# Converting the float64 weights of a fused kernel: sign on GpSimd, low bits as 16-bit halves, one subtraction moved

## The chip, the cores and the metric

The kernel runs on one core of one Trainium2 chip. Its time is device microseconds of one execution; the figure for a kernel is the median of several runs. A trace taken by the hardware profiler on one execution lies beside the times, and all rows below come from it. The engines are TensorE (PE for its matmuls, PEld for its weight loads), VectorE (DVE), ScalarE (ACT), GpSimd (POOL) and SyncE (SP, which issues most DMAs).

## The reference

Three layers follow one another. Linear attention over 8 batches, 8 heads, 576 positions and 64 channels: a softmax of q over channels, a softmax of k over positions, `kv = k^T v`, then `q kv`. The result, 4608 tokens of 512 channels, goes through a feed-forward layer: `h = x @ w_in` (512 to 2048), `g = s * relu(h)^2 + b`, `y = g @ w_out` (2048 to 512). Then a mixture of 8 experts: each token goes to the one expert with the highest cosine similarity, through `relu(x @ w1[e]) @ w2[e]`, times its softmax weight.

What matters here: `w_in` and `w_out` arrive as float64. No engine of this kernel works in float64, so the kernel itself turns every weight into a float32 by bit operations on its two 32-bit words: the sign is the top bit of the high word, exponent and the first 20 mantissa bits come from the high word, and the last three mantissa bits are the top three bits of the low word.

## The kernel before

Work is in blocks. The feed-forward layer runs over 12 token tiles of 384 (index `t`) and, inside each, over 16 blocks of 128 hidden columns (index `m`). Per block, `emit_l1` (lines 483 to 485) multiplies each weight tile three times, high part by high, high by low, low by high, because a float32 is split into two parts `fp32r`, a rounded high part and the rest. `emit_g` squares and scales on ScalarE (lines 496 to 509), `emit_l2` (lines 524 to 528) multiplies by `w_out`. In the first tile, `t = 0`, blocks 0 to 13 take `w_out` unsplit: line 524 reads the converted float32 weights, the tile named `cxout`, directly. Only from block 14 on is the split pair (`wout`) read, lines 526 to 528.

Weights are converted while `t = 0` runs. There are 16 pieces of 128x1024 values, eight of `w_in` (`in 0` to `in 7`) and eight of `w_out`, in the order in 0, in 1, out 0, in 2, out 1, and so on. A piece takes these instructions:

- `conv_load`: SP loads the raw float64 words, two loads of 512 KB, into the tile `rawin` or `rawout`.
- `conv_a`: ScalarE takes the absolute value of the high word and rescales it into `ct` (line 162); VectorE shifts the low word right by 29 and writes all 32 bits of `x` (line 163), then writes the sign into the upper 16-bit half of `x` (line 164). `x` is the tile `cxin` or `cxout`, of which there are two each.
- `conv_b`: VectorE shifts `ct` left by three and ORs it with `x` (line 171), ScalarE rounds the result to the high part (line 175).
- `conv_c`: VectorE subtracts the high part to get the low part (line 179).

`conv_first` does this for in 0 inside the opening section, where attention of batch 0 and tile 0 is computed. `conv_step` does it for the others: at each `m` of tile 0, half 0 issues a load and `conv_b` of the piece before, half 1 issues `conv_a` of the next piece and `conv_c` of the piece before.

Beside this, attention for the next tile and batch is computed in small steps by generators (`attn_k`, `attn_q`), in places fixed by tables. In `attn_k` VectorE reduces a maximum (lines 255 to 262), PE transposes it (line 267), VectorE reduces again (line 270), PE spreads it back (line 273), VectorE subtracts it (lines 292 and 294), ScalarE takes the exponential (lines 299 and 300) and PE multiplies by v (line 311). Each engine runs its instructions in the order in which the program issues them; an instruction that waits holds up all that stand behind it on its engine. `consts_late`, at the end of tile 0, fills small constants and the token table on GpSimd (lines 117 to 138).

Of the kernel before, what the change touches and what calls it, by code (L numbers as in the profile page):

```python
# [8 lines left out]
F32 = mybir.dt.float32  # L9
F32R = mybir.dt.float32r  # L10
BF16 = mybir.dt.bfloat16
I32 = mybir.dt.int32
U16 = mybir.dt.uint16
ALU = mybir.AluOpType
# [11 lines left out]
NM = DFF // 128  # L26
# [23 lines left out]

GLB = 2
IDLE = {(1, 0): 26}
LATE = {(7, 2): 1, (6, 3): 2, (2, 1): 1, (5, 3): 2, (7, 0): 2, (4, 1): 2, (6, 1): 2, (5, 2): 2, (1, 1): 2, (4, 3): 1, (3, 1): 2, (7, 3): 2, (3, 0): 1, (2, 0): 2, (1, 3): 1}


@with_exitstack
def attn_ffn_moe(ctx: ExitStack, tc: tile.TileContext, q, k, v, w_in, w_out, s_in, b_in,
                 emb, tau, w1, w2, out, ysc=None):
    nc = tc.nc
# [13 lines left out]
    sp = stage.enter_context(tc.tile_pool(name="sp", bufs=2, side="right"))  # L73
# [11 lines left out]
    def wpair(dtype, name):  # L85

        return wp.tile([128, 2, 1024], dtype, tag="w", name=name)
# [53 lines left out]
    wt = {}  # L141
    raw_t = {}
    conv_t = {}
    full = {}

    def conv_load(kind, i):

        r = wpair(I32, f"raw{kind}{i}")
        for n in range(2):
            nc.sync.dma_start(out=r[:, n, :], in_=(w_in if kind == "in" else w_out)[2 * i + n])  # L150
        raw_t[kind, i] = r

    def conv_a(kind, i):

        t = sp.tile([128, 1024], I32, tag="ct", name="ct", bufs=1)
        room = "in" if (kind, i) == ("out", NM // 2 - 1) else kind
        x = sp.tile([128, 1024], I32, tag="cx" + room, name="cx" + kind)
        raw = raw_t.pop((kind, i)).rearrange("p n c -> p (n c)")
        r = raw.rearrange("p (f two) -> p f two", two=2)
        r16 = raw.bitcast(U16).rearrange("p (f four) -> p f four", four=4)  # L160
        x16 = x.bitcast(U16).rearrange("p (f two) -> p f two", two=2)
        nc.scalar.activation(out=t.bitcast(F32), in_=r[:, :, 1].bitcast(F32), func=AF.Abs, scale=2.0 ** -112)
        nc.vector.tensor_scalar(out=x, in0=r[:, :, 0], scalar1=29, scalar2=None, op0=ALU.logical_shift_right)
        nc.vector.tensor_scalar(out=x16[:, :, 1], in0=r16[:, :, 3], scalar1=0x8000, scalar2=None,
                                op0=ALU.bitwise_and)
        conv_t[kind, i] = (t, x)

    def conv_b(kind, i):

        t, x = conv_t.pop((kind, i))  # L170
        nc.vector.scalar_tensor_tensor(out=x, in0=t, scalar=3, in1=x,
                                       op0=ALU.logical_shift_left, op1=ALU.bitwise_or)
        full[kind, i] = x.bitcast(F32)
        wt[kind, i] = wpair(F32R, f"w{kind}{i}")
        nc.scalar.activation(out=wt[kind, i][:, 0, :], in_=full[kind, i], func=AF.Copy)

    def conv_c(kind, i):
        w = wt[kind, i]
        nc.vector.tensor_tensor(out=w[:, 1, :], in0=full[kind, i], in1=w[:, 0, :].bitcast(F32), op=ALU.subtract)

    def w_of(kind, m):

# [45 lines left out]
    def idle(n, o=None):  # L228

        if o is None:  # L230
            o = ps_h()
        z = ident.bitcast(BF16)
        for _ in range(n):
            nc.tensor.matmul(o[:, 256:512], z[:, 0:128], z, start=True, stop=True)
# [13 lines left out]
    def attn_k(b, j, kt, vt, dg, after=None, ke=None):  # L248
# [53 lines left out]
        if b > KP:  # L302
            yield
        for _ in range(LATE.get((b, j), 0)):
            yield
        pk = bank()
        idle(IDLE.get((b, j), 0), pk)
        for r in range(5):
# [703 lines left out]
    with tc.manual_schedule():  # L1012
# [10 lines left out]
        order = [("in", 0)]  # L1023
# [13 lines left out]
        nc.sync.dma_start(out=b_sb, in_=b_in.partition_broadcast(128))  # L1037
        conv_i = [1]

        def conv_first():  # L1040
            yield
            conv_a(*order[0])
            yield
            conv_b(*order[0])
            yield
            yield
            conv_c(*order[0])

        def conv_step(half):

            i = conv_i[0]
            if i > len(order):
                return
            if half == 0:
                if loads:
                    conv_load(*loads.pop(0))
                if i > 1:
                    conv_b(*order[i - 1])
            else:
                if i < len(order):  # L1060
                    conv_a(*order[i])
                if i > 1:
                    conv_c(*order[i - 1])
                conv_i[0] += 1
# [58 lines left out]
        start_pairs(-16)  # L1123
        line = {f"{w}{j}": act[4 * i + j] for i, w in enumerate("kq") for j in range(4)}
        line["c"] = conv_first()
        act.clear()
        start_pairs(-2)
        line["K"], line["Q"] = act
        for w in ("f32 q0 q0 k0 k1 k1 k0 k0 q0 f4 k0 k0 f4 q0 q0 k1 q1 k0 f5 k1 k2 q1 f5 k0 k1 k2 k2 k1 q2 f4 k2 q1 q2 k2 "
                  "f7 q1 k0 c q2 k1 q1 k3 q2 k2 q0 c q3 q2 k3 q0 w w k2 k0 q3 k3 k1 c k3 q1 k1 c k3 q3 f12 q3 q1 c "  # L1130
                  "k3 q3 k3 k2 q0 k2 k3 q2 q1 k3 q2 k0 K q3 q3 q2 K q3 Q C Q k1 k2 k3").split():
            if w == "w":
                conv_load(*loads.pop(0))
            elif w[0] == "f":
                idle(int(w[1:]))
            elif w == "C":
                conv_step(0)
                conv_step(1)
            else:
                next(line[w], None)  # L1140
# [98 lines left out]
        for t in range(NB):  # L1239
            for m in range(NM + (LAG if t == NB - 1 else 0)):  # L1240
# [15 lines left out]
                if t == 0:  # L1256
                    go(4)
                    conv_step(0)
                elif m % 2 == 0 or not pairs:
                    go(2)  # L1260
# [128 lines left out]
        n = nc.values_load(ut_box[1][0:1, UT_N:UT_N + 1], min_val=0, max_val=NB2)  # L1389
# [22 lines left out]
def build(arrays, debug=False):  # L1412
    import concourse.bacc as bacc

    nc = bacc.Bacc("TRN2", target_bir_lowering=False, num_devices=1)
    args = [nc.dram_tensor(n, a.shape, mybir.dt.from_np(a.dtype), kind="ExternalInput").ap()
            for n, a in arrays.items()]
    out = nc.dram_tensor("out", (NT, DM), F32, kind="ExternalOutput").ap()
    ysc = nc.dram_tensor("ysc", (NT + 1, DM), F32, kind="ExternalOutput").ap() if debug else None
    with tile.TileContext(nc) as tc:  # L1420
        attn_ffn_moe(tc, *args, out, ysc)
    return nc
# [38 lines left out]
```

## Time and profile before

| | |
|---|---|
| median of 3 runs | 1318.36 us (1318.25 to 1318.7) |
| profiled execution, its own time | 1320.52 us |
| its span from first to last instruction | 1318.8 us |
| TensorE busy | 1299.3 us, 99% |
| VectorE busy | 914.2 us, 69% |
| ScalarE busy | 795.6 us, 60% |
| GpSimd busy | 140.4 us, 11% |

The busy shares are means over the whole span. The conversion touches only its first 115 us: its first vector instruction starts at 17.8 us and its last ends at 114.3 us. In that part VectorE is busy about 90% of the time and GpSimd almost not at all. The chain of waits on the page says little about it, since it follows the last instruction back only a few steps. So the part is read from the timeline of each engine and from the waits in that stretch.

### The profile page before, as it was taken

What the parts mean: (1) busy time and instruction counts of PE and PEld (TensorE: products, weight loads), DVE (VectorE), ACT (ScalarE), POOL (GpSimd) and SP (SyncE); (2) the same over time, 40 slices, a digit from 0 to 9 for tenths busy, and PEclk for the clock granted to TensorE, in tenths of its full rate; (3) what the DMA queues carried; (4) which work ended last, traced back from release to release, by engine and by line L of the source; (5) the groups of instructions that cost most, each with busy time, mean ns of one, the idle gap of its engine ahead of it and who ended that gap; (6) DMA issues with size and microseconds to landing.
All of it is one profiled execution on the core that took longest, in us unless ns stands there. A gap on an engine that the chain in (4) does not pass through costs nothing. (4 is left out here: it accounts for less than half of the span.)

```text
span 1318.8 us, 20627 instructions
## 1 busy us (share of the span) xinstructions
PE 1299.3 (99%) x6997; PEld 1116.8 (85%) x6997; DVE 914.2 (69%) x2546; ACT 795.6 (60%) x1684; POOL 140.4 (11%) x161
## 2 busy tenths in 40 slices
PE   7999999999999999999999999999999999999997
PEld 5668988989889988988989999998878888888885
DVE  7997897888777878788777777456769344444430
ACT  6788766776767676676867766656334343434331
POOL 0000001010100000000001001011313221121101
PEclk9999999999999999999999999999999999999999
DMA  8753312121211121111212010332222233424521
GB/s 243 265 195 87 89 40 58 36 55 31 66 31 55 31 52 41 55 36 31 55 48 49 19 31 7 105 111 54 88 61 70 76 88 98 168 78 137 184 97 36
DMA packets 106246, 104.08 MB, mean 79 GB/s; under 512 B 54480, under 2 KB 82384, under 8 KB 106130
## 3 DMA queue, kind: packets, MB, share of 16 engines
q1 hardware_dynamic: 99058, 83.48, 22.0%
q0 software_dynamic: 7072, 19.18, 4.4%
q8 instruction: 57, 0.93, 0.3%
q14 instruction: 59, 0.48, 0.2%
HBM read 103.06 MB, written 19.47 MB: 93 GB/s over the span
## 5 line engine op out<-in xcount | busy, mean ns | idle before, releaser
L483 PE MATMUL ps_h<-xth,win 128*128 128x384 f32 x768 | 260.5, 339 | 1.6 <-ACT r L496 1.6
L485 PE MATMUL ps_h<-xth,win 128*128 128x384 f32 x768 | 257.7, 336 | 0.0
L484 PE MATMUL ps_h<-xtl,win 128*128 128x384 f32 x768 | 257.1, 335 | 0.0
L527 PE MATMUL ps_y<-wout,gl 128*128 128x512 f32 x534 | 209.6, 392 | 1.2 <-DVE gl L511 1.0
L526 PE MATMUL ps_y<-wout,gh 128*128 128x512 f32 x534 | 210.1, 393 | 0.2 <-ACT gh L509 0.2
L528 PE MATMUL ps_y<-wout,gh 128*128 128x512 f32 x534 | 209.3, 392 | 0.0
L603 DVE CUSTOM_DVE_ANT_0 scr<-ysb,eb 128x512 bf16<-128x512 f32 x264 | 180.3, 683 | 2.5
L511 DVE TENSOR_TENSOR gl<-r,gh 128x384 fp32r<-128x384 f32 x178 | 98.6, 554 | 104.0 <-ACT gh L509 102.1
L509 ACT ACTIVATE gh<-r 128x384 fp32r<-128x384 f32 x178 | 93.4, 525 | 97.7 <-PE ps_y L528 93.9
L483 PEld LDWEIGHTS ps_h<-xth,win 128*128 128x128 f32 x768 | 144.4, 188 | 6.5 <-ACT r L496 2.4
L484 PEld LDWEIGHTS ps_h<-xtl,win 128*128 128x128 f32 x768 | 144.3, 188 | 2.6 <-issue 0.2
L485 PEld LDWEIGHTS ps_h<-xth,win 128*128 128x128 f32 x768 | 144.1, 188 | 0.0
L505 ACT ACTIVATE r<-r,b_sb,s_sb 128x384 f32<-128x384 f32 x178 | 126.3, 709 | 5.9
L496 ACT ACTIVATE r<-ps_h 128x384 f32<-128x384 f32 x192 | 92.5, 482 | 52.7 <-DVE gl L511 25.1
L527 PEld LDWEIGHTS ps_y<-wout,gl 128*128 128x128 f32 x534 | 100.2, 188 | 21.7 <-DVE gl L511 2.9
L528 PEld LDWEIGHTS ps_y<-wout,gh 128*128 128x128 f32 x534 | 100.2, 188 | 21.3
L526 PEld LDWEIGHTS ps_y<-wout,gh 128*128 128x128 f32 x534 | 100.3, 188 | 20.1 <-ACT gh L509 0.6
L728 DVE TENSOR_TENSOR l<-r,h 128x1024 fp32r<-128x1024 f32 x72 | 87.7, 1220 | 41.6 <-ACT h L727 41.5
L775 DVE SCALAR_TENSOR_TENSOR hl<-ps_h,hh 128x512 fp32r<-128x512 f32 x71 | 49.0, 690 | 96.6 <-ACT hh L774 96.6
L768 PE MATMUL ps_h<-xh,h 128*128 128x512 f32 x288 | 112.4, 390 | 0.4 <-DVE hl L775 0.4
L769 PE MATMUL ps_h<-xl,h 128*128 128x512 f32 x288 | 112.1, 389 | 0.0
L770 PE MATMUL ps_h<-xh,l 128*128 128x512 f32 x288 | 112.0, 389 | 0.0
(318 smaller groups left out, 2229.9 us busy)
## 6 DMA issues: line engine op xcount, KB each, us to landing
r<-moe_w SPq DMA_DIRECT2D x80, 512.0 KB
ysc<-ysb SPq DMA_DIRECT2D x36, 256.0 KB
x<-xr SPq DMA_DIRECT2D x288, 32.0 KB
qt_s<-q SPq DMA_DIRECT2D x45, 192.0 KB
rawin<-moe_w_in SPq DMA_DIRECT2D x16, 512.0 KB
rawout<-moe_w_out SPq DMA_DIRECT2D x16, 512.0 KB
kt_s<-k SPq DMA_DIRECT2D x29, 256.0 KB
vt_s<-v SPq DMA_DIRECT2D x29, 256.0 KB
```

What stands on the lines that cost most here:

```text
L483: nc.tensor.matmul(hp, wh[:, ws], xth[i][:, kk, :], start=(kk == 0), stop=False)
L484: nc.tensor.matmul(hp, wh[:, ws], xtl[i][:, kk, :], start=False, stop=False)
L485: nc.tensor.matmul(hp, wl[:, ws], xth[i][:, kk, :], start=False, stop=(kk == KC - 1))
L505: nc.scalar.activation(out=r, in_=r, func=AF.Identity, scale=s_sb, bias=b_sb)
L511: nc.vector.tensor_tensor(out=l, in0=r, in1=g.bitcast(F32), op=ALU.subtract)
L526: nc.tensor.matmul(y, g[:, cs], wh, start=(m == 0), stop=False)
L527: nc.tensor.matmul(y, l[:, cs], wh, start=False, stop=False)
L528: nc.tensor.matmul(y, g[:, cs], wl, start=False, stop=(m == NM - 1))
L603: nc.vector.tensor_tensor_reduce(out=junk_box[-1], in0=yt, in1=eb[:, e, :], scale=1.0, scalar=0.0, op0=ALU.mult, op1=ALU.add, accum_out=dt ...
L768: nc.tensor.matmul(o, wh, xh[:, kk, :], start=(kk == 0), stop=False)
L769: nc.tensor.matmul(o, wh, xl[:, kk, :], start=False, stop=False)
L770: nc.tensor.matmul(o, wl, xh[:, kk, :], start=False, stop=(kk == KC - 1))
```

## The change

GpSimd gets a new first instruction for each piece, `conv_p`: it multiplies the high word, read as a float32, by 0.0. That gives plus or minus zero, so all 32 bits of `x` are written and only the sign bit can be set. VectorE then no longer shifts 32-bit words and no longer writes the sign; one instruction on 16-bit halves shifts the upper half of the low word right by 13 and writes the lower half of `x`. For the pieces out 1 to out 7 the subtraction of `conv_c` runs on GpSimd; out 0 and all of `w_in` stay on VectorE.

```diff
+SUB = ('out',)
...
+    def conv_p(kind, i):
         room = "in" if (kind, i) == ("out", NM // 2 - 1) else kind
         x = sp.tile([128, 1024], I32, tag="cx" + room, name="cx" + kind)
+        h = raw_t[kind, i].rearrange("p n c -> p (n c)").rearrange("p (f two) -> p f two", two=2)[:, :, 1]
+        nc.gpsimd.tensor_scalar(out=x.bitcast(F32), in0=h.bitcast(F32), scalar1=0.0, scalar2=None, op0=ALU.mult)
+        conv_x[kind, i] = x
...
-        nc.vector.tensor_scalar(out=x, in0=r[:, :, 0], scalar1=29, scalar2=None, op0=ALU.logical_shift_right)
-        nc.vector.tensor_scalar(out=x16[:, :, 1], in0=r16[:, :, 3], scalar1=0x8000, scalar2=None,
-                                op0=ALU.bitwise_and)
+        nc.vector.tensor_scalar(out=x16[:, :, 0], in0=r16[:, :, 1], scalar1=13, scalar2=None,
+                                op0=ALU.logical_shift_right)
...
     def conv_c(kind, i):
         w = wt[kind, i]
-        nc.vector.tensor_tensor(out=w[:, 1, :], in0=full[kind, i], in1=w[:, 0, :].bitcast(F32), op=ALU.subtract)
+        eng = nc.gpsimd if kind in SUB and i > 0 else nc.vector
+        eng.tensor_tensor(out=w[:, 1, :], in0=full[kind, i], in1=w[:, 0, :].bitcast(F32), op=ALU.subtract)
...
+        conv_p(*order[0])
         def conv_first():
...
             if half == 0:
                 if loads:
                     conv_load(*loads.pop(0))
+                if i < len(order):
+                    conv_p(*order[i])
                 if i > 1:
                     conv_b(*order[i - 1])
```

`conv_p` stands half a step ahead of `conv_a` of the same piece. The added lines shift the line numbers: line 164 becomes 172, line 171 becomes 179, line 179 becomes 188, line 270 becomes 279, line 292 becomes 301, and the new GpSimd instruction is line 160.

VectorE, before, around the pieces in 1 (`rawin_154`) and out 0 (`rawout_370`), in the first block of tile 0:

```order
L342 TENSOR_REDUCE qs<-qt_s 128x6
L163 TENSOR_SCALAR cxin<-rawin_154 128x1024
L164 TENSOR_SCALAR cxin<-rawin_154 128x1024
L329 TENSOR_TENSOR kvl_98<-d_1_120,kvh_96 128x128
...
L270 TENSOR_REDUCE cm<-ps_a 128x1
L171 SCALAR_TENSOR_TENSOR cxin<-ct,cxin 128x1024
L416 TENSOR_SCALAR qr<-qr 128x6
L417 RECIPROCAL qr<-qr 128x6
L419 TENSOR_TENSOR qt_s<-qt_s,qr 128x2x3x64
L163 TENSOR_SCALAR cxout<-rawout_370 128x1024
L164 TENSOR_SCALAR cxout<-rawout_370 128x1024
L179 TENSOR_TENSOR win_507<-cxin,win_507 128x1024
L292 TENSOR_TENSOR kt_s<-kt_s,ps_a 128x2x4x64
```

The same place in the changed kernel:

```order
L351 TENSOR_REDUCE qs<-qt_s 128x6
L172 TENSOR_SCALAR cxin<-rawin_154 128x1024
L338 TENSOR_TENSOR kvl_98<-d_1_120,kvh_96 128x128
...
L279 TENSOR_REDUCE cm<-ps_a 128x1
L179 SCALAR_TENSOR_TENSOR cxin<-ct,cxin 128x1024
L425 TENSOR_SCALAR qr<-qr 128x6
L426 RECIPROCAL qr<-qr 128x6
L428 TENSOR_TENSOR qt_s<-qt_s,qr 128x2x3x64
L172 TENSOR_SCALAR cxout<-rawout_370 128x1024
L188 TENSOR_TENSOR win_509<-cxin,win_509 128x1024
L301 TENSOR_TENSOR kt_s<-kt_s,ps_a 128x2x4x64
```

One instruction a piece has left VectorE; what remains stands in the same order. Two pieces lie between the first row and the last, so two instructions have gone ahead of the subtraction of the maximum.

GpSimd, before, after its opening fills (`v_3_125` is a tile of v); nothing of the conversion stands there:

```order
L1021 MEMSET v_3_125 128x10x2
L117 MEMSET onesb 128x128
L119 AFFINE_SELECT tri<-onesb 128x128
L121 IOTA tok 128x36
L123 IOTA ci 128x8
L124 CAST eidx<-ci 128x8
```

In the changed kernel (the first seven new ones, and then the last one, of out 7):

```order
L1030 MEMSET v_3_125 128x10x2
L160 TENSOR_SCALAR cxin<-rawin_146 128x1024
L160 TENSOR_SCALAR cxin<-rawin_154 128x1024
L160 TENSOR_SCALAR cxout<-rawout_370 128x1024
L160 TENSOR_SCALAR cxin<-rawin_373 128x1024
L160 TENSOR_SCALAR cxout<-rawout_477 128x1024
L160 TENSOR_SCALAR cxin<-rawin_503 128x1024
L188 TENSOR_TENSOR wout_689<-cxout,wout_689 128x1024
...
L188 TENSOR_TENSOR wout_1216<-cxout,wout_1216 128x1024
L118 MEMSET onesb 128x128
L120 AFFINE_SELECT tri<-onesb 128x128
```

16 sign instructions and 7 subtractions now stand on GpSimd ahead of the constants of `consts_late`.

## Rows read from the trace of the kernel before

**Rows 1.** The page, TensorE's busy time and its share of the span.

```profile
PE 1299.3 (99%) x6997; PEld 1116.8 (85%) x6997; DVE 914.2 (69%) x2546; ACT 795.6 (60%) x1684; POOL 140.4 (11%) x161
```

**Rows 2.** Busy time by stretch: engines, then TensorE's clock, DMA share, GB/s.

```profile
30.00:40.00 10.00, 8.37 (x74) 7.21 (x73) 9.83 (x19) 6.48 (x19) 0.00 (x0) 1.00 1.02 406
60.00:70.00 10.00, 10.00 (x62) 7.19 (x61) 9.33 (x17) 7.88 (x13) 0.00 (x0) 1.00 0.57 164
```

**Rows 3.** Timeline of TensorE: start, duration, engine, line, [idle before, releaser].

```profile
29.02 0.33 PE L267 MATMUL ps_a<-ident,dg_s 128*128 128x128 f32 x1 [1.78 <-DVE dg_s L262]
...
32.58 0.32 PE L273 MATMUL ps_a<-ident,cm 128*128 128x128 f32 x1 [1.11 <-DVE cm L270]
...
38.36 0.95 PE L311 MATMUL ps_a<-vt_s,kt_s 128*64 128x66 f32 x20 [0.52 <-ACT kt_s L299]
...
56.79 0.44 PE L483 MATMUL ps_h<-xth,win 128*128 128x384 f32 x1 [1.56 <-ACT r L496]
...
77.95 0.95 PE L311 MATMUL ps_a<-vt_s,kt_s 128*64 128x66 f32 x20
...
119.90 0.40 PE L528 MATMUL ps_y<-wout,gh 128*128 128x512 f32 x1
```

**Rows 4.** Timeline of VectorE, 27 to 38 us.

```profile
27.90 0.43 DVE L255 TENSOR_TENSOR scr<-kt_s 128x256 f32<-128x256 f32 x1 [0.96 <-DMA kt_s<-k]
...
30.29 0.68 DVE L163 TENSOR_SCALAR cxin<-rawin 128x1024 int32<-128x1024 int32 x1
31.00 0.75 DVE L164 TENSOR_SCALAR cxin<-rawin 128x1024 uint16<-128x1024 uint16 x1
31.64 0.68 DVE L329 TENSOR_TENSOR kvl<-d,kvh 128x128 fp32r<-128x128 f32 x3
32.24 0.28 DVE L270 TENSOR_REDUCE cm<-ps_a 128x1 f32<-128x128 f32 x1
...
34.48 0.69 DVE L163 TENSOR_SCALAR cxout<-rawout 128x1024 int32<-128x1024 int32 x1
...
36.97 0.68 DVE L292 TENSOR_TENSOR kt_s<-kt_s,ps_a 128x512 f32<-128x512 f32 x1
```

**Rows 5.** Lines 163 and 179: durations min/median/max in ns, first and last start.

```profile
L163 DVE TENSOR_SCALAR cxin<-rawin x8: 677/688/691, 17.8 to 94.5; 128x1024 int32<-128x1024 int32 x8
...
L179 DVE TENSOR_TENSOR wout<-cxout,wout x8: 1198/1208/1227, 41.2 to 113.1; 128x1024 fp32r<-128x1024 f32 x8
```

**Rows 6.** Timeline of ScalarE.

```profile
17.59 1.16 ACT L162 ACTIVATE ct<-rawin 128x1024 f32<-128x1024 f32 x1 [0.68 <-DMA rawin<-moe_w_in]
...
51.58 1.06 ACT L175 ACTIVATE wout<-cxout 128x1024 fp32r<-128x1024 f32 x1 [0.86 <-DVE cxout L171]
...
77.57 0.30 ACT L300 ACTIVATE kt_s<-kt_s 64x128 f32<-64x128 f32 x1
```

**Rows 7.** Timeline of GpSimd: small reads, a fill, a power, a copy.

```profile
103.63 0.92 POOL L124 CAST eidx<-ci 128x8 f32<-128x8 int32 x1
...
105.25 0.20 POOL L127 TENSOR_SCALAR desc<-eidx 128x8 f32<-128x8 f32 x1
...
111.88 0.38 POOL L136 MEMSET pf<- 128x292 int32 x1 [5.77 <-DVE cxout L171]
...
168.79 2.32 POOL L566 TENSOR_TENSOR nr<-es,half 128x8 f32<-128x8 f32 x1 [56.24 <-DVE es L565]
...
907.00 1.17 POOL L858 COPY eb<-eidx 1x8 f32<-1x8 f32 x1
```

**Rows 8.** Timeline of VectorE beside those rows of GpSimd.

```profile
103.27 1.23 DVE L171 SCALAR_TENSOR_TENSOR cxout<-ct,cxout 128x1024 int32<-128x1024 int32 x1
...
169.00 0.54 DVE L511 TENSOR_TENSOR gl<-r,gh 128x384 fp32r<-128x384 f32 x1
...
905.75 2.37 DVE L728 TENSOR_TENSOR l<-r,h 128x1024 fp32r<-128x1024 f32 x2 [0.26 <-ACT h L727]
```

**Rows 9.** The DMA issue of SP behind the token table.

```profile
121.86 0.34 SPq L225 DMA_DIRECT2D qt_s<-q  x1
```

More of the change, by code (lines that the diff above doesn't have):

```diff
@@ L143, in attn_ffn_moe @@
     conv_t = {}
+    conv_x = {}
     full = {}
@@ L151, in conv_load @@
         raw_t[kind, i] = r
+    def conv_p(kind, i):
+        room = "in" if (kind, i) == ("out", NM // 2 - 1) else kind
+        x = sp.tile([128, 1024], I32, tag="cx" + room, name="cx" + kind)
+        h = raw_t[kind, i].rearrange("p n c -> p (n c)").rearrange("p (f two) -> p f two", two=2)[:, :, 1]
+        nc.gpsimd.tensor_scalar(out=x.bitcast(F32), in0=h.bitcast(F32), scalar1=0.0, scalar2=None, op0=ALU.mult)
+        conv_x[kind, i] = x
     def conv_a(kind, i):
         t = sp.tile([128, 1024], I32, tag="ct", name="ct", bufs=1)
-        room = "in" if (kind, i) == ("out", NM // 2 - 1) else kind
-        x = sp.tile([128, 1024], I32, tag="cx" + room, name="cx" + kind)
+        x = conv_x.pop((kind, i))
         raw = raw_t.pop((kind, i)).rearrange("p n c -> p (n c)")
```

## Prediction

> **What bounds the kernel.** The page first: TensorE is busy 1299.3 of 1318.8 us [rows 1], so the whole of its idle time is 19.5 us, and work taken from another engine can win only what TensorE waits for. Next, the busy time by stretch, to see where it waits. While weights are converted TensorE is full from 60 us on (10.00 of 10.00) although VectorE is at 9.33; between 30 and 40 us TensorE is at 8.37 and VectorE at 9.83 [rows 2]. So VectorE is the bound only in the first block or two of tile 0. Last, TensorE's own timeline with its waits. From the first converted piece on, those of note are 1.78 us at 29.02, 1.11 at 32.58, 0.52 at 38.36 and 1.56 at 56.79 [rows 3]. The rest of the span is behind these and moves only as a block.
>
> Each wait has to be followed to what ends last. The one at 29.02 is not VectorE's work: VectorE itself sat 0.96 us idle at 27.90 until the load of `kt_s` landed [rows 3, 4]. That landing is an anchor. What VectorE gains ahead of it is lost, and what it loses there is free up to 0.96 us. The one at 32.58 waits for the reduction of line 270, which started at 32.24 behind both conversion instructions of piece in 1 [rows 3, 4]. The one at 38.36 waits for ScalarE's exponential, which waits for the subtraction of line 292 at 36.97, and that stands behind the instructions of out 0 as well [rows 3, 4]. The one at 56.79 is ScalarE's: its queue is filled through, and it had waited for VectorE once, 0.86 us at 51.58 [rows 3, 6].
>
> **What is removed.** Line 163 goes 16 times (two rows of eight, one shown, at 688 ns), and line 179 seven times at 1208 ns [rows 5]. That is 11.0 + 8.5 = 19.5 us of VectorE's time. Nearly all of it lies where TensorE does not wait. On the path, from the anchor at 27.90 to line 292, stand two of the 16: piece in 1 at 30.29, and out 0 at 34.48. The next instruction starts 0.71 us after the first of them [rows 4], so the path gets 2 x 0.71 = 1.42 us shorter. The 16-bit shift that stays has the shape of line 164 (16-bit in at a stride, 16-bit out at a stride), so I price it as that one, 31.00 to 31.64, 0.64 us [rows 4], no change.
>
> Does 1.42 us reach TensorE? At 32.58 its wait is 1.11, so the first 0.71 comes through and 0.40 is left. At 38.36 another 0.52 is there to win; 0.71 + 0.52 = 1.23. The remaining 0.19 comes through later, since VectorE and ScalarE then hand on to each other with waits, and the wait at 56.79 is longer than that. Behind line 292 the two engines run in lockstep; the subtraction of out 0 (`i = 0`) stays on VectorE, so nothing more leaves that path before 51.58. Whole gain on the path: 1.42 us.
>
> **What is added.** The trace shows no GpSimd instruction on 1024 columns. From below: a fill of 292 columns takes 0.38 us [rows 7]; at that pace throughout, 1024 columns take 1.3, and if 0.2 us of it is fixed, as a read of 8 columns costs [rows 7], 0.2 + 1024 x 0.18 / 292 = 0.8. From above I take twice VectorE's longest pass over the same tile, 2 x 1.2 = 2.4 [rows 5]. I take 1.2 for a sign pass, near the fill. A subtraction reads two tiles: bounds 1.2 (VectorE's own row) and 3 x 1.3 = 3.9 (two reads and a write, one after another), taken 2.2.
>
> The Trainium skill (GPSIMD Engine Reference, Performance versus the Vector engine) has 4497 ns for a two-input addition of 2048 float32 on GpSimd; half of it, as an estimate, is 2.25 us. By that figure the sum below stays as it is.
>
> *Waiting for the sign.* VectorE's shift now waits for GpSimd. For in 0 the raw words land at 17.59, when ScalarE's wait for them ends [rows 6]. The pass ends at 18.8, the shift 0.64 later at 19.4; before, both instructions were through at 17.8 + 0.71 + 0.64 = 19.15 [rows 4, 5]. That is 0.3 us late, 1.5 with a pass of 2.4, and behind it wait the reductions of q and k of the fourth head pair. The cover is the 0.96 us at 27.90: cost 0, at most 0.5. For out 0 I work out the landing: after `kt_s` at 27.90 come two loads of 512 KB, 1.05 MB at the 406 GB/s of [rows 2], 2.6 us, and up to 0.45 MB of v and q ahead of them, 1.1 us: 30.5 to 31.6. With a pass of 1.2 the sign is there by 32.8; it is wanted at 34.48 - 0.71 = 33.8. Cover 1.0 us; with 2.4 it is 0.2 late.
>
> *Room on GpSimd.* The out pieces follow each other every (113.1 - 41.2) / 7 = 10.3 us [rows 5]. In that time GpSimd has two sign passes and one subtraction: 2 x 1.2 + 2.2 = 4.6, at the upper bounds 8.7. It keeps up.
>
> *The end of tile 0.* The last subtraction, of out 7, cannot start before about 113 us (line 179 ran to 113.1 + 1.2). With 2.2 us it ends near 115.3; the first matmul that reads a low part of `w_out` is at 119.90 [rows 3], cover 4.6. All constants of `consts_late` now queue behind it on GpSimd. The second fill of the token table, which ended soon after 111.88 [rows 7], comes some 6 us later, and SP holds its DMA that long; SP's next entry is at 121.86 [rows 9], so nothing behind it is late.
>
> *The port.* Here is the unknown that decides. GpSimd's cast of 8 columns at 103.63 took 0.92 us where a like read takes 0.20; it ended at 104.55, VectorE's two-input instruction at 104.50. A copy at 907.00 took 1.17 and ended at 908.17, VectorE's pair at 908.12 [rows 7, 8]. So GpSimd's reads stand still while VectorE reads two tiles from SBUF. The other direction isn't there: a GpSimd power of 2.32 us from 168.79 ran beside a VectorE subtraction at 169.00 that took its usual 0.54 [rows 7, 8]. But it reads 8 columns, and the new passes read 1024. So a pass can hold VectorE for nothing (that row) or for its whole length. Near the path lie the passes of out 0, in 2 and out 1. Bounds 0 and 3 x 1.2 = 3.6; I take half of one pass, 0.6, since the row at hand says none.
>
> The Trainium skill (SBUF — State Buffer, Who interferes with whom) says that a VectorE instruction with two SBUF inputs and a GpSimd instruction that reads SBUF exclude each other, and that the second to issue "fully blocks". The trace agrees for GpSimd as the second (0.92 us for 0.20). By that rule GpSimd as the first would hold VectorE as well, and the time is that of the first rival.
>
> **Sum.** -1.42 + 0 (in 0) + 0 (out 0) + 0 (end) + 0.6 = -0.8 us. The profiled execution took 1320.52 us, 1.7 more than its span; by the sum it would be 1319.7. The median of the runs lies 2.2 lower, at 1318.36, and the same sum gives 1317.6.
>
> **Rivals.**
>
> *VectorE is held: slower.* Each sign pass that runs beside VectorE's two-input work keeps it waiting for the pass. It takes back what it brings once a pass holds VectorE longer than the 0.71 us that it removes. Place: from 30.5 us on, the passes of out 0, in 2 and out 1, which all land before line 292. Price 3.6 - 1.42 = +2.2. Later a subtraction of 2.2 us can do the same, where margins are thin: at 77.95 TensorE's line 311 starts with ScalarE's exponential ended only 0.08 before, at 77.87 [rows 3, 6]. Half a subtraction once, +1.1 there. Together +3.3: 1321.7. For it: GpSimd's waits, VectorE at 9.83 of 10. Against: the power, and that VectorE has 19.5 us freed to absorb holds after 60 us.
>
> *All waits shrink: faster.* If the ports do not collide and ScalarE, served earlier, also frees the wait of 1.56 us at 56.79, then -1.42 - 1.56 = -3.0: 1315.4. For it: ScalarE waited 0.86 for VectorE at 51.58. Against: the other 0.7 is ScalarE's own queue, and the steps behind line 292 run in lockstep.
>
> *The sign comes too late: the change does not relieve VectorE.* With passes of 2.4 and more VectorE stands at the shift for as long as line 163 took. in 0 costs 0.5 beyond its cover, out 0 0.2; the gain in piece in 1 stays, 0.71, and out 0's is gone. About 0: 1318.4. Against: the fill's pace.
>
> **Chances.** Forecast 0.50, held VectorE 0.24, all waits 0.13, late sign 0.13. A measurement of this kernel can tell about 0.2%, 2.6 us, from no change. Faster by more takes the second rival and a little of the forecast: 0.15. Slower takes most of the first rival, and a little of the forecast and the third: 0.23. Within: 0.62. The range goes from the second rival to just beyond the first, 1315.3 to 1322.2. The forecast's own range, with both pieces' gain and none or two passes held, is 1316.9 to 1319.3.
>
> **What would show it.** Right: TensorE's wait at line 273 in the first block falls from 1.11 to about 0.4, that at line 311 nearly vanishes, that at 56.79 stays over 1 us; VectorE's conversion shift waits for GpSimd only at in 0; 60 us and after stay without waits; the sign passes last 1.0 to 1.5 us. Wrong: VectorE's two-input instructions lengthen, or gaps appear before them while a pass runs (first rival); sign passes of over 2 us and VectorE idle at line 172 for most pieces (third); the wait at 56.79 gone (second). A change of more than 4 us either way would mean that something outside the first 115 us has moved, which this working has no place for.

## The result and the profile after

| | before | after |
|---|---|---|
| median | 1318.36 us (1317.49 to 1318.77) | 1327.16 us (1323.71 to 1328.57) |
| ratio to before, 95% interval | | 1.0064 (1.0049 to 1.0079) |
| profiled execution, span | 1320.52, 1318.8 us | 1326.68, 1325.0 us |

The change is slower, by 8.8 us in the medians of five runs each, and the forecast of 1317.6 was wrong in sign. The two profiled executions lie 6.2 us apart, because the one of before was 2.2 us above its median and the one of after 0.5 below. What follows goes by these two traces. At 135 us the changed kernel is 7.1 us behind before; after that the profiled execution of before loses about 1 us itself, which leaves the 6.2. It loses 0.4 to 2.4 us there against every other kernel traced below, so this part belongs to that one execution and not to the change. Of the 8.8 some 7.1 us are thus placed, and 1.7 are in no trace.

The page of after, engine line, answers to [rows 1]:

```profile
PE 1300.8 (98%) x6997; PEld 1117.2 (84%) x6997; DVE 909.2 (69%) x2523; ACT 795.3 (60%) x1684; POOL 206.8 (16%) x184
```

Here is the first surprise. The change takes 11.0 us of line 163 and 7 x 1.21 = 8.5 us of line 179 off VectorE [rows 5], 19.5 together, and VectorE's busy time fell by only 5.0. Some 14.5 us have come back in instructions that were there before. The stretches, to be read against [rows 2] (the columns are those of that view):

```profile
30.00:40.00 10.00, 7.74 (x52) 6.72 (x52) 9.86 (x18) 5.71 (x16) 9.07 (x3) 1.00 1.02 408
90.00:100.00 10.00, 9.13 (x39) 5.98 (x38) 7.91 (x12) 7.56 (x13) 8.17 (x3) 1.00 0.32 124
```

Between 30 and 40 us VectorE is as full as before (9.86 against 9.83) with one instruction fewer, GpSimd is busy 9 us of 10, and TensorE has lost 0.6. Between 90 and 100 TensorE is at 9.13, where before had 9.74, with VectorE far from full. Where TensorE waits, from its timeline (line 276 was 267, 282 was 273, 320 was 311, 492 was 483), against [rows 3] and three more rows of before:

```profile
30.72 0.33 PE L276 MATMUL ps_a<-ident,dg_s 128*128 128x128 f32 x1 [0.73 <-DVE dg_s L271]
33.56 0.32 PE L282 MATMUL ps_a<-ident,cm 128*128 128x128 f32 x1 [0.40 <-DVE cm L279]
41.31 0.95 PE L320 MATMUL ps_a<-vt_s,kt_s 128*64 128x66 f32 x20 [2.45 <-ACT kt_s L308]
...
59.67 0.45 PE L492 MATMUL ps_h<-xth,win 128*128 128x384 f32 x1 [1.51 <-ACT r L505]
...
81.86 0.95 PE L320 MATMUL ps_a<-vt_s,kt_s 128*64 128x66 f32 x20 [0.94 <-ACT kt_s L308]
94.73 0.30 PE L276 MATMUL ps_a<-ident,dg_s 128*128 128x128 f32 x1 [0.87 <-DVE dg_s L271]
105.70 0.95 PE L320 MATMUL ps_a<-vt_s,kt_s 128*64 128x66 f32 x20 [1.24 <-ACT kt_s L308]
...
135.45 0.95 PE L320 MATMUL ps_a<-vt_s,kt_s 128*64 128x66 f32 x20
```

Before:

```profile
89.32 0.27 PE L267 MATMUL ps_a<-ident,dg_s 128*128 128x128 f32 x1
...
99.27 0.95 PE L311 MATMUL ps_a<-vt_s,kt_s 128*64 128x66 f32 x20 [0.26 <-ACT kt_s L299]
...
128.36 0.95 PE L311 MATMUL ps_a<-vt_s,kt_s 128*64 128x66 f32 x20
```

The lag behind before at the same instruction is 1.70 us at the first row, 0.98 at the second, 2.95 at the third, 2.88 at the fourth and 3.91 at 81.86 (before 77.95). The next two stood at 89.32 and 99.27 before, which makes 5.41 and 6.43, and the last at 128.36, which makes 7.09. So the loss has four places: 1.7 ahead of the first row, 1.25 in the first block, some 3.5 from 60 to 106 us, where the prediction expected no wait at all, and 0.7 up to 135 us.

GpSimd's groups of the conversion in after (busy us, mean ns | idle before):

```profile
L160 POOL TENSOR_SCALAR cxin<-rawin 128x1024 f32<-128x1024 f32 x8 | 26.8, 3344 | 19.1 <-DMA rawin<-moe_w_in 19.1
L160 POOL TENSOR_SCALAR cxout<-rawout 128x1024 f32<-128x1024 f32 x8 | 23.7, 2968 | 3.9 <-DMA rawout<-moe_w_out 3.9
L188 POOL TENSOR_TENSOR wout<-cxout,wout 128x1024 fp32r<-128x1024 f32 x7 | 16.7, 2379 | 30.9 <-ACT wout L183 30.9
```

A sign pass takes about 3 us, not 1.2, and is longer than the subtraction, which reads twice as much and takes the 2.4 that it was priced at (2.2). Now GpSimd's timeline, with one pass alone and some beside VectorE:

```profile
17.81 2.85 POOL L160 TENSOR_SCALAR cxin<-rawin 128x1024 f32<-128x1024 f32 x1 [15.58 <-DMA rawin<-moe_w_in]
24.16 2.86 POOL L160 TENSOR_SCALAR cxin<-rawin 128x1024 f32<-128x1024 f32 x1 [3.49 <-DMA rawin<-moe_w_in]
...
33.75 3.63 POOL L160 TENSOR_SCALAR cxin<-rawin 128x1024 f32<-128x1024 f32 x1
37.34 3.31 POOL L160 TENSOR_SCALAR cxout<-rawout 128x1024 f32<-128x1024 f32 x1
...
57.93 2.84 POOL L160 TENSOR_SCALAR cxout<-rawout 128x1024 f32<-128x1024 f32 x1
...
113.01 2.37 POOL L188 TENSOR_TENSOR wout<-cxout,wout 128x1024 fp32r<-128x1024 f32 x1 [2.58 <-ACT wout L183]
```

And VectorE's timeline over the same time, against [rows 4]:

```profile
20.70 0.74 DVE L172 TENSOR_SCALAR cxin<-rawin 128x1024 uint16<-128x1024 uint16 x1 [2.96 <-POOL cxin L160]
...
24.56 0.74 DVE L391 TENSOR_SCALAR qr<-qr 128x6 f32<-128x6 f32 x1
...
29.60 0.42 DVE L264 TENSOR_TENSOR scr<-kt_s 128x256 f32<-128x256 f32 x1
...
34.56 1.11 DVE L425 TENSOR_SCALAR qr<-qr 128x6 f32<-128x6 f32 x1
...
36.40 1.57 DVE L172 TENSOR_SCALAR cxout<-rawout 128x1024 uint16<-128x1024 uint16 x1
37.88 2.11 DVE L188 TENSOR_TENSOR win<-cxin,win 128x1024 fp32r<-128x1024 f32 x1
39.92 0.67 DVE L301 TENSOR_TENSOR kt_s<-kt_s,ps_a 128x512 f32<-128x512 f32 x1
...
58.56 1.56 DVE L179 SCALAR_TENSOR_TENSOR cxin<-ct,cxin 128x1024 int32<-128x1024 int32 x1 [2.71 <-ACT ct L171]
60.04 0.76 DVE L425 TENSOR_SCALAR qr<-qr 128x6 f32<-128x6 f32 x1
...
113.16 2.37 DVE L338 TENSOR_TENSOR kvl<-dg_s,kvh 128x128 fp32r<-128x128 f32 x1 [0.73 <-ACT kvh L335]
```

Three things are to be seen. First, VectorE stands idle 2.96 us at 20.70 for the sign of in 0. Second, from 34.56 on three instructions are long: line 425 by 0.94 us over its usual 0.17, line 172 by 0.82 over 0.75, line 188 by 0.90 over 1.21. Nothing is idle between them; the wait is inside the instruction. Third, line 301, whose second input comes from PSUM, has its usual length though GpSimd's pass beside it ran until 40.65. The instruction with the largest stretch is a small one: line 338, on 128 columns, lasts as long as GpSimd's subtraction beside it.

These holds have a pattern. Take the end of a long instruction, less its usual duration, as the moment at which it really began. At 58.56 that is 58.56 + 1.56 - 1.21 = 58.91, 1.86 us before the end of the pass (57.93 + 2.84 = 60.77). At 60.04 it is 60.63, 0.14 before that end. Of the 20 VectorE instructions in after that are over 0.2 us too long, 17 lie beside sign passes. Ten of them began 1.85 to 1.89 us before a pass's end, three (all of line 428) 2.12 to 2.13, and four 0.14 to 0.15; beside subtractions all three began 0.14 before the end. So a sign pass stops VectorE in two stretches of up to about 0.9 us, with a free one between them, and a subtraction stops it throughout.

The two stretches stop different instructions. Count, in all eight kernels here with sign passes (or, in one of them, passes like them), the VectorE instructions that read and write SBUF alone. Of those that start in the last 0.2 to 0.99 us of a pass, all 25 with two inputs kept their length, and 21 of the 22 `tensor_scalar` (one input and a constant) were held. Of those that start in its first 0.8 us, 44 of 49 with two inputs were held and 16 of 21 `tensor_scalar`; the ten others stand beside passes that were themselves stretched, to 3.4 us and more. A plain fill of 0.95 us on GpSimd, in two of the kernels below, treats VectorE like the last stretch: it held 5 `tensor_scalar` of 5 and none of 44 with two inputs. So the pattern looks like a pass that first reads and at its end only writes. That is a reading of the pattern; no run takes a pass apart.

The same by groups, in the first 125 us. Before:

```profile
L164 DVE TENSOR_SCALAR cxout<-rawout 128x1024 uint16<-128x1024 uint16 x8 | 6.2, 772 | 0.3
...
L419 DVE TENSOR_TENSOR qt_s<-qt_s,qr 128x384 f32<-128x384 f32 x4 | 2.2, 558 | 0.1
...
L329 DVE TENSOR_TENSOR kvl<-dg_s,kvh 128x128 fp32r<-128x128 f32 x5 | 1.5, 291 | 1.9 <-ACT kvh L326 1.9
...
L416 DVE TENSOR_SCALAR qr<-qr 128x6 f32<-128x6 f32 x4 | 0.7, 166 | 0.0
```

After:

```profile
L172 DVE TENSOR_SCALAR cxout<-rawout 128x1024 uint16<-128x1024 uint16 x8 | 7.8, 970 | 0.2 <-POOL cxout L160 0.2
...
L338 DVE TENSOR_TENSOR kvl<-dg_s,kvh 128x128 fp32r<-128x128 f32 x5 | 4.6, 921 | 2.6 <-ACT kvh L335 2.6
L428 DVE TENSOR_TENSOR qt_s<-qt_s,qr 128x384 f32<-128x384 f32 x4 | 4.2, 1046 | 0.1
L425 DVE TENSOR_SCALAR qr<-qr 128x6 f32<-128x6 f32 x4 | 3.4, 846 | 0.0
```

These four alone gave back 1.6 + 3.1 + 2.0 + 2.7 = 9.4 us. The excess of all 20 sums to 14.1, nearly the 14.5 of the page.

### The profile page after: what moved, and what is told of

It reads as the page before. It is cut to its first block, busy times and chain, and to the rows that moved or that the text cites. A ratio compares the mean times of both kernels' runs of the same rounds, so it can differ in the third digit from the quotient of the medians.

```text
span 1325.0 us, 20657 instructions
## 1 busy us (share of the span) xinstructions
PE 1300.8 (98%) x6997; PEld 1117.2 (84%) x6997; DVE 909.2 (69%) x2523; ACT 795.3 (60%) x1684; POOL 206.8 (16%) x184
## 5 line engine op out<-in xcount | busy, mean ns | idle before, releaser
L535 PEld LDWEIGHTS ps_y<-wout,gh 128*128 128x128 f32 x534 | 100.3, 188 | 19.5
```

The lines of the kernel that those rows point to most:

```text
L535: nc.tensor.matmul(y, g[:, cs], wh, start=(m == 0), stop=False)
```

## The experiments

The theory after the result: GpSimd's reads hold VectorE. Its rivals: the sign simply comes late, because a pass is long; the moved subtractions do it; in 0 alone does it. In the kernels below a list `SIGN` names the pieces whose sign GpSimd makes; the others keep the two VectorE instructions of before. Before took 1318.58, 1318.41 and 1318.46 us on the chips used, and each ratio is to before on the same chip.

**Signs alone.** All subtractions back on VectorE.

```diff
-SUB = ('out',)
+SUB = ()
```

> The sign passes stay on GpSimd; all subtractions go back to VectorE. In the changed kernel TensorE is behind the kernel before by 1.7 us at the start of tile 0 (line 267 before), 2.9 at line 311 of block one, 3.9, 5.4 and 6.4 at the later waits (78, 89 and 99 us before). Theory A (the two engines hold each other in SBUF, whichever issues second waits): the first two stay, +1.7 and +2.9, and of the later 3.5 us some 2 stay, since sign passes are 5.7 of the 8.1 us of GpSimd time in two blocks: span +5 us over before. Theory B (GpSimd's results only come late, no hold): later loss comes from the subtractions' place, so it is gone: +2.9 at every later anchor, span +3.

Measured: 1324.33 us, ratio 1.0041 (1.0027 to 1.0055). VectorE's busy time is 913.8 us, 0.4 below before, though 11.0 us of line 163 are gone: 10.6 came back. Behind before it was by 2.0 us at the start, 4.1 at line 311 of block one (2.9 expected) and 5.5 from 99 us on. The sign passes alone make the kernel slower and relieve VectorE of next to nothing.

**Subtractions alone.** The conversion of before, out 1 to out 7 subtracted on GpSimd.

```diff
+SIGN = ()
```

> The conversion of before with its two VectorE instructions; only the subtractions of out 1 to 7 run on GpSimd. Theory A (hold): nothing at the start and in block one (first GpSimd subtraction at about 53 us), later VectorE instructions with two SBUF inputs that stand beside a subtraction last up to 2.4 us; VectorE loses seven times 1.2 us of work but is held about as long: span +0 to +2 us, 1318.4 to 1320.5. Theory B (no hold): VectorE has 8.5 us less to do and TensorE waits as before: 1318.0 to 1318.4.

Measured: 1319.03 us, ratio 1.0003 (0.9993 to 1.0013), no difference to be told. GpSimd's and VectorE's timelines of this kernel show the hold all the same (line 200 is the subtraction, 350 was 329):

```profile
105.18 2.39 POOL L200 TENSOR_TENSOR wout<-cxout,wout 128x1024 fp32r<-128x1024 f32 x1 [7.60 <-ACT wout L195]
```

```profile
105.34 2.39 DVE L350 TENSOR_TENSOR kvl<-dg_s,kvh 128x128 fp32r<-128x128 f32 x1 [0.80 <-ACT kvh L347]
```

The hold is not free. It makes ScalarE, which next waits for VectorE at 112.13, 0.97 us late, and TensorE, 0.61 us ahead of before at 98.66 (line 332), is 0.03 ahead at 128.33. But 0.6 us of 8.8 is little, and the median shows no difference, so the subtractions alone fall as the main cause.

**In 0 back.** As after, but in 0 converted by VectorE as before.

```diff
+SIGN = [p for p in order if p != ('in', 0)]
```

> As the changed kernel, but piece in 0 alone is converted by VectorE with the two instructions of before. If VectorE's wait of 2.96 us for the first sign is what puts tile 0 1.7 us late (and TensorE at its lower clock from 20 to 26 us), line 267 starts at 29.0 again and the span is 1.5 to 1.9 us under the changed kernel's; if the delay comes from the passes behind it (in 1 beside VectorE's work), line 267 stays about 30.7.

Measured: 1324.56 us, ratio 1.0047 (1.0031 to 1.0064). TensorE's timeline (line 288 was 267, 332 was 311):

```profile
29.27 0.33 PE L288 MATMUL ps_a<-ident,dg_s 128*128 128x128 f32 x1 [1.86 <-DVE dg_s L283]
40.00 0.95 PE L332 MATMUL ps_a<-vt_s,kt_s 128*64 128x66 f32 x20 [1.66 <-ACT kt_s L320]
```

The start's delay is gone: 29.27 against 29.02 before and 30.72 after. The loss in the first block stays: 29.27 to 40.00 is 10.73, before 9.34 [rows 3]. In 0 accounts for 1.5 to 2.6 us (by that matmul, or by the medians, whose intervals overlap) and not for the rest. This share is lateness, VectorE's wait of 2.96 us, and hangs on when the raw words land: in the run with early signs below the pass of in 0 began at 16.94 in place of 17.81, and VectorE waited 1.32.

**Fill instead of sign.** The sign is left out: GpSimd fills `x` with zeros, without reading; everything else is as after.

```diff
-        nc.gpsimd.tensor_scalar(out=x.bitcast(F32), in0=h.bitcast(F32), scalar1=0.0, scalar2=None, op0=ALU.mult)
+        nc.gpsimd.memset(x.bitcast(F32), 0.0)
```

> The sign pass is replaced with a fill of zeros on GpSimd of the same tile, so the sign of the weights is left out and GpSimd reads nothing there; subtractions as in the changed kernel. Theory A, with a hold between GpSimd's reads and VectorE's second input: VectorE's two-input instructions beside a fill keep 1.2 us, block one loses nothing (line 311 within 0.5 us of before plus the start's delay); the fill lasts 1.1 to 1.4 us, so in 0 waits 1.3 instead of 2.96. Span +1 to +3 over before, all of it behind 60 us. If any GpSimd instruction holds VectorE whether it reads or not, block one stays late by about 1 us. Theory B (lateness): the shorter fill takes the start's delay away and the rest with it: span within 0.5 us of before.

Measured: 1317.43 us, ratio 0.9992 (0.9982 to 1.0002). A fill takes 0.95 us. VectorE's timeline, from the landing of `kt_s`, the prediction's anchor (line 276 was 255), to the subtraction of the maximum (313 was 292):

```profile
28.02 0.43 DVE L276 TENSOR_TENSOR scr<-kt_s 128x256 f32<-128x256 f32 x1 [1.41 <-DMA kt_s<-k]
...
35.65 0.69 DVE L313 TENSOR_TENSOR kt_s<-kt_s,ps_a 128x512 f32<-128x512 f32 x1
```

It is 7.63 us, against 36.97 - 27.90 = 9.07 before [rows 4]. So the relief of 1.42 us is real once nothing takes it back: measured 1.44. The span is below what either theory expected; it is not told from before. But a fill is also short and early, so this run doesn't part a hold from a late sign.

**A late, long GpSimd that doesn't read the piece.** Sign left out again; GpSimd waits for the raw words by reading 8 columns and then fills `x` three times.

```diff
+        nc.gpsimd.tensor_scalar(out=x.bitcast(F32)[:, 0:8], in0=h.bitcast(F32)[:, 0:8], scalar1=0.0, scalar2=None, op0=ALU.mult)
+        for _ in range(3):
+            nc.gpsimd.memset(x.bitcast(F32), 0.0)
```

> The sign pass is replaced with a read of 8 columns, which waits for the raw words, and three fills of the whole tile (0.95 us each in the run with one fill), so it comes as late and lasts about as long, 3.0 us, as the sign pass, but reads almost nothing; the sign is left out, the subtractions stay on GpSimd. If reading is what holds VectorE: in 0 still waits about 3 us and puts the start 1.5 us late, but no VectorE instruction from 30 us on lasts longer than usual, line 311 of block one is not later than the start's delay (1.5), and the later loss of 3.4 us is gone: span +0 to +1.5 over before. If lateness and length are the cause, reading or not: as the changed kernel, +2.9 at line 311, span +5 to +6.5.

Measured: 1319.36 us, ratio 1.0005 (0.9996 to 1.0015). Its VectorE, same place (line 439 was 416, 186 is the shift, 315 was 292):

```profile
32.98 0.90 DVE L439 TENSOR_SCALAR qr<-qr 128x6 f32<-128x6 f32 x1
...
34.90 0.77 DVE L186 TENSOR_SCALAR cxout<-rawout 128x1024 uint16<-128x1024 uint16 x1 [0.20 <-POOL cxout L165]
...
36.70 0.67 DVE L315 TENSOR_TENSOR kt_s<-kt_s,ps_a 128x512 f32<-128x512 f32 x1
```

The three fills last 2.98 us, like a pass, and VectorE does wait for them, 3.7 us over the whole conversion; they even stretch the 128x6 instruction. But beside the fills the instructions with two inputs keep their length, and the kernel is not measurably slower than before. With the same GpSimd time ahead of the shift, the pass over 1024 columns in place of the fills is what separates 1.0005 from 1.0064, or from 1.0047 without in 0 (in this run in 0 waited only 0.16 us, as its 8 columns came with half of the load). In the changed kernel itself line 172 waits for a sign at two of the 16 pieces, 2.96 us at in 0 and 0.17 at 95.89. Lateness is not enough; the hold stands. Whether it is the reading or the multiplication that holds, this run doesn't part: no pass here multiplies without reading.

**A pass that reads half the bytes, side by side.** Sign left out: the same multiplication on 1024 contiguous 16-bit halves (`r_` is the raw tile as one row).

```diff
-        nc.gpsimd.tensor_scalar(out=x.bitcast(F32), in0=h.bitcast(F32), scalar1=0.0, scalar2=None, op0=ALU.mult)
+        nc.gpsimd.tensor_scalar(out=x.bitcast(F32), in0=r_.bitcast(U16)[:, 0:1024], scalar1=0.0, scalar2=None, op0=ALU.mult)
```

> The sign pass reads the first 1024 16-bit halves of the raw tile, side by side, in place of the 1024 high words at a stride of 8 bytes; the signs it writes are not the weights' signs. If the stride (or the bytes read) makes a pass 2.85 us, it gets near the fill's 0.95 to 1.3 us; if the arithmetic on 1024 columns does, it stays at 2.8 to 2.9 us, and the span with it.

Measured once: 1323.58 us; the `out` pieces' passes by groups:

```profile
L164 POOL TENSOR_SCALAR cxout<-rawout 128x1024 f32<-128x1024 uint16 x8 | 23.1, 2885 | 4.6 <-DMA rawout<-moe_w_out 4.6
```

2885 ns against 2968: neither the stride nor the width makes the pass long. The holds stay, 22 instructions by 14.5 us in all. In this run, too, in 0 came early (VectorE waited 0.39 us for it), as in the one with three fills; one execution can't give a verdict, but its TensorE is 4.9 us behind before at 135 us, that of the three fills 0.75.

**Early and late signs.** The first six pieces' signs on GpSimd, subtractions on VectorE; then the other ten's; then the other ten's with the subtractions of out 1 to out 7.

```diff
+SIGN = order[:6]   # early;   late: order[6:]
-SUB = ('out',)     # early and late; late with subtractions keeps it
+SUB = ()
```

> Signs of the first six pieces only (in 0, in 1, out 0, in 2, out 1, in 3) on GpSimd, all else as before. Counted from TensorE's line 267 at the start of tile 0 to its line 311 in block one, before takes 9.3 us, the changed kernel 10.6. If the holds belong to the passes beside that block, it is 10.6 here too, the start is 1.5 to 2 us late, and nothing is lost behind 57 us: median +2.5 to +3.5 over before. If late holds are what carries the loss, +1 or less.

> Signs of the other ten pieces (out 2 to out 7) on GpSimd, the first six and all subtractions as before. The start and block one are as before (9.3 us). Between 57 and 106 us TensorE had no slack in the changed kernel: it lost 3.5 us there, with the subtractions on GpSimd too. If the sign passes alone make that, +3 to +3.5; if it takes both, about +1 as in the run with all signs and no subtraction.

> As the run before in this call, and the subtractions of out 1 to 7 on GpSimd: all that the changed kernel does behind 50 us, and nothing ahead of it. If the parts add up, the loss is the 3.5 us of the changed kernel behind 57 us, median 1321.5 to 1322.2; if the late loss hangs on the late start, +1 or less.

Measured: 1322.31 us (ratio 1.0033, 1.0020 to 1.0046), 1320.50 (1.0014, 1.0004 to 1.0023) and 1322.20 (1.0030, 1.0019 to 1.0041). Early is 3.85 us, late 2.0, late with subtractions 3.7; subtractions alone had been 0.45. Early and late with subtractions sum to 7.6 of the 8.8. Late signs and subtractions together cost 1.2 more than the sum of each alone, less than the intervals can tell; in the traces TensorE loses 1.2 us from line 267 to 135 us with late signs, 0.9 with subtractions and 4.6 with both. The early kernel's trace doesn't show its loss: the profiled execution was the fastest of six (1320.30 us), its start is 0.4 us late and block one loses 0.5, where 1.5 to 2 and 1.3 were expected. TensorE's timeline of the third kernel shows the place of the late loss:

```profile
78.48 0.95 PE L332 MATMUL ps_a<-vt_s,kt_s 128*64 128x66 f32 x20 [0.81 <-ACT kt_s L320]
91.34 0.30 PE L288 MATMUL ps_a<-ident,dg_s 128*128 128x128 f32 x1 [0.84 <-DVE dg_s L283]
102.32 0.95 PE L332 MATMUL ps_a<-vt_s,kt_s 128*64 128x66 f32 x20 [1.24 <-ACT kt_s L320]
```

They are the three waits of after at 81.86, 94.73 and 105.70. With late signs alone the first is 0.24, the second is absent and the third 1.07.

**What the profile points to.** VectorE's conversion of out 0 stands ahead of line 292, which does not need it, so it was issued behind line 294, with nothing on GpSimd; and then the sign of in 1 was given to GpSimd as well, whose pass (25.21 to 28.07) lies in a stretch where VectorE waits for the load.

```diff
+        later.append(low)      # out 0: lines 163 and 164
...                             # behind the subtraction of the maximum:
+        for f in later: f()
```

> The conversion of before, without GpSimd; only the two VectorE instructions of piece out 0 (lines 163 and 164) are issued later, behind lines 292 and 294, just ahead of line 171 of that piece. If the first block is bound by VectorE's order, line 292 starts 1.35 us earlier, the wait of 0.52 at line 311 goes, and about 0.8 of the waits behind it: 1.0 to 1.3 us faster, 1317.2 to 1317.5. If ScalarE's queue sets that stretch, no change.

> As the run before in this call, and the sign of piece in 1 alone on GpSimd: its pass starts when the raw words land at about 24 us and ends at 27, before VectorE's wait for the load of kt_s ends at 27.9, so holds are covered by 0.96 us of idle time there. Line 270 in block one starts 0.71 us earlier; 0.7 us on top: 1316.5 to 1316.9. If the pass holds VectorE beyond its cover (5 to 6 instructions with two SBUF inputs stand there), nothing is won, 1317.3 or later.

Measured: 1317.94 us, ratio 0.9997 (0.9988 to 1.0006), and 1317.84, ratio 0.9996 (0.9987 to 1.0005). Both fall short of what was expected, 1.0 to 1.3 us and 0.7 more. TensorE's waits in the second kernel's first block (299 was 267, 515 was 483):

```profile
29.31 0.33 PE L299 MATMUL ps_a<-ident,dg_s 128*128 128x128 f32 x1 [1.84 <-DVE dg_s L294]
...
56.20 0.45 PE L515 MATMUL ps_h<-xth,win 128*128 128x384 f32 x1 [1.53 <-ACT r L528]
```

The waits at lines 273 and 311 are gone, and the stretch is 26.89 us against 27.77 before [rows 3], 0.88 shorter. That is below what the runs can tell, and the landing of `kt_s` moves the whole by as much (line 255 starts at 26.84 in the profiled execution of the first kernel and at 28.19 in that of the second). No version here beats before measurably.

## Why the prediction was wrong

Three steps failed: the price of a sign pass, the port term that rests on it, and the reading that 60 us and after have no waits. The path, the relief on it and the price of a subtraction came out as predicted.

**The relief: right; what bounds the kernel: half right.** The path from the landing of `kt_s` to line 292 was the one that counts in block one, and it does get 1.42 us shorter (1.44 with fills); TensorE's wait at line 273 fell to 0.40 as forecast. But that VectorE bounds only the first block or two was read off one row, 60 to 70 us. Between 90 and 100 TensorE had 9.74 of 10, with a wait of 0.26 at 99.27.

**The price of a sign pass: wrong, and its upper bound too.** Taken 1.2 us, bounds 0.8 to 2.4; measured 2.85 with VectorE idle beside it (17.81) and up to 4.66 in company. The bounds came from a fill, which reads nothing (0.95 here for 1024 columns), and from twice a VectorE pass, which says nothing about GpSimd. The subtraction's price was right (2.2, measured 2.38). The Trainium skill (GPSIMD Engine Reference, Engine selection) calls one-input work on GpSimd "roughly line-rate". This trace does not agree: one input takes longer than two.

**In 0 at no cost: wrong, by that price.** Worked out again with 2.85: the shift is through at 20.70 + 0.64 = 21.34 instead of 19.15, 2.2 late; the cover of 0.96 takes its part; the pass of in 1 then holds line 391 for 0.57 more (24.56). 2.2 - 0.96 + 0.57 = 1.8; measured 1.70. Of the lag, most is the late sign, the place of the third rival.

**The port term: wrong.** Taken 0.6 over the passes of out 0, in 2 and out 1 near the path; measured 0.94 + 0.82 + 0.90 = 2.66 there, all beside the last two (out 0's, from 30.93, held nothing). Relief and hold give -1.42 + 2.66 = +1.24; line 264 to line 301 takes 10.32 us after, 9.07 before: +1.25. I leaned on the row of the power that ran beside a VectorE subtraction of the usual length [rows 7, 8]. That row has 8 columns to read, and a row on 8 columns is no evidence for 1024. The rival "VectorE is held" had the mechanism, the place and the point of decision, a pass that holds VectorE for more than the 0.71 it frees. With signs alone a pass gave back 10.6 / 16 = 0.66 us of the 0.69 that it removes, so almost nothing was freed; on the path the two pieces removed 1.42 and the holds took 2.66.

**"60 us and after stay without waits": wrong.** VectorE has room there on average, and that was taken for cover. But most of the holds fall on the attention chain: from 57 us on 8.6 of 10.9 us on lines 425 and 428 for q, 264 and 265 for the maximum, 338 for `kv`. They make VectorE's later work late by more than the removed instructions give back, and that reaches TensorE through ScalarE, which takes its work in order and stands at line 183 until VectorE's conversion has finished a piece. That wait was there before, too, and grew (line 183 was 175):

```profile
68.06 1.06 ACT L175 ACTIVATE win<-cxin 128x1024 fp32r<-128x1024 f32 x1 [1.06 <-DVE cxin L171]
```

```profile
72.15 1.06 ACT L183 ACTIVATE win<-cxin 128x1024 fp32r<-128x1024 f32 x1 [2.54 <-DVE cxin L179]
```

ScalarE's exponential of line 308 stands behind it, and TensorE waits for that at 81.86. The prediction's margin there counted ScalarE's end 0.08 us before TensorE's start, but not what ScalarE itself waited for. The rival put +1.1 at line 311 at 77.95, and it was +1.0 there; 1.5 and 1.0 more followed at the next two waits, and 0.7 behind them, after line 338 was held 2.08 us by a subtraction (113.16).

**The rival's size.** It had +3.3 where the traces show 7.1: 1.7 for in 0, 1.25 in block one, about 3.5 up to 106 us and 0.7 behind. A late sign and a hold stood in two different rivals, each priced as if the other did not happen, and the later hold was counted once. The first two places share one cause, a pass more than twice as long as assumed; in the later ones passes and subtractions act together. Nor does a change of more than 4 us mean, as the last sign had it, that something outside the first 115 us has moved: 6.4 of the 7.1 lie inside them.

What stays open: whether the reading or the multiplication is what holds VectorE in the first stretch of a pass, why late signs and subtractions together cost more than each alone, where the early signs' 3.85 us arise, and the 1.7 us of the medians' difference that no trace shows.

## What to carry to other kernels

Work given to idle GpSimd is not free if it reads or writes SBUF beside a full VectorE: count what VectorE gets back in longer instructions, not what leaves its list. Price an operation on another engine by a row of that engine with as many columns and as many reads; where there is none, the upper bound has to be far away, and every term that rests on it moves with it. And look at which instructions stand beside the new one: a delay that falls on a short instruction of a critical chain comes through to the engine that waits for it, however much room the held engine has on average.

## What the runs showed of the hardware

- GpSimd's multiplication of 1024 columns by a constant takes 2.85 us alone from 32-bit words at a stride and 2.77 to 2.80 from contiguous 16-bit halves; its two-input subtraction 2.37, a fill 0.95.
- VectorE's instructions with two SBUF inputs, and `tensor_scalar` from SBUF to SBUF, lengthen beside a GpSimd subtraction or sign pass (128x128 from 0.29 to 2.37 us, 128x6 from 0.17 to 1.11); line 301, with an input from PSUM, doesn't (0.67). GpSimd's pass lengthens too, to as much as 4.66. The Trainium skill (SBUF — State Buffer, Who interferes with whom) has the first to issue hold the ports for its whole instruction. The subtraction agrees (VectorE began 0.14 us before its end, three times of three); the sign pass doesn't, since VectorE ran in the middle of it, and with two inputs at its end too (25 of 25).
- Fills lengthen a 128x6 `tensor_scalar` as well (0.90 against 0.17), but not two-input instructions (none of 44; line 202 took 1.20 us at 35.57 beside fills).
- TensorE's granted clock fell to 0.50, the 1.2 GHz level, early in both kernels: over 17.0 to 20.4 us before and 19.4 to 26.2 us after. In the 5 us ahead of the fall TensorE had been busy 3.26 us before and 2.44 after. The wait for in 0's sign lies in that stretch. No cost of it shows on VectorE's path: its lag behind before is 2.17 us at 21.33 and 2.16 at 24.56.
